# Dealing the first chunk's q and k by groups of heads from two weight halves, and packing attention output two heads a transfer

## The chip, the cores and the metric

One core of one Trainium2 chip runs the kernel. The metric is device time in microseconds (us): the median of three runs was 587.67 (585.95 to 587.77). A separate, profiled execution took 589.12 and left the trace that is read here.

## The reference, cut to what matters

`x` is 2048 rows of 576 numbers (bf16). It is normalised row by row, and two branches are added to it:

```python
xn = _layernorm(x)
# A: sliding-window attention, 32 heads of 18, each query sees itself and the 255 keys before it
qkv = (xn @ wqkv).reshape(B, S, 3, 32, 18)
o = softmax(mask(q @ k.T * 18 ** -0.5)) @ v
a = o.reshape(B, S, 576) @ wo
# B: gated feed-forward, 4608 wide
b = (silu(xn @ w1) * (xn @ w3)) @ w2
out = x + a + b
```

## The kernel before, in words

**Chunks and units.** The 2048 rows are worked in four chunks of 512 (loop at L869). A chunk has a projection stage (q, k and v of its rows), a first phase of 36 *units*, and a second phase that multiplies by w2 and wo and stores the result. Unit u (`unit_pairs` L691, `unit_tanh` L706, `unit_h` L712) makes 128 columns of the gated feed-forward with 18 matmuls (L700), a tanh on ScalarE (L709) and two operations on VectorE (L715, L718). Between the units' matmuls lie the attention's score steps (`scores` L589, `exps` L601, `masks` L608), and three times in a chunk a `pv` (L634) that multiplies the exponentials by v for two groups of heads; the fourth `pv` lies in the second phase. A group is four heads; there are eight groups. TensorE's instructions are in one written order, so a unit whose weights are late holds up all that follows it.

**Weights by fills.** The columns of w1 and w3 come in *fills*: fill k holds 512 columns, serves four units, and is six transfers of 192 KB (`load_part` L314, its DMA L325). There are three buffers, and fill 3 goes into a part of `hT` that is not in use yet. Unit 4 of the first chunk needs all of fill 1, unit 8 all of fill 2, unit 12 fill 3, unit 16 fill 4, unit 20 fill 5, unit 32 fill 8. `load_w13` (L330) issues six transfers at once. `owed` is a debt of transfers: `owe_part` (L337) pays one of them after the fourth and one after the ninth pair of matmuls of a unit, and that transfer waits for the matmul just issued. So a debt of six made before unit u is paid in units u to u+2. w2 comes through `load_w2` (L345, DMA L352).

**The queue of SyncE (SP).** Nearly all transfers are issued by SP, in program order: x tiles (L301), weights (L325, L352), the moves that deal q and k (L527 in the first chunk, L555 later), the attention output (L685), wo (L994, L996) and the results (L766). A transfer that waits for something holds up all that is written after it in this queue. ScalarE (ACT) issues a few transfers as well.

**Dealing q and k.** A projection leaves q and k with columns of the weight matrix on the partitions, 128 to a row tile of `stage` (nine tiles). The score matmuls want, for each group of four heads, two pairs of heads on partitions 0 to 35 and 64 to 99, in `qv` and `kv`. DMAs do this move. From the second chunk on the weights in `wp` are dealt by groups beforehand: row tile g holds the 72 q columns and 54 of the 72 k columns of group g, the remaining 18 k columns of seven groups lie in tile 8, and those of one group in rows 126 and 127 of all tiles. `repack_span` (L532) then moves several groups with one transfer: two for q, three for k, and one for each group's remainder (two for the spread group). In the first chunk the projection uses the weights as they stand in memory (`wa`, which lies over the buffers `pt`; `w8` is a copy of some of its columns): q and k columns in order, so that a head may cross from one tile to the next. `pieces` (L487) cuts every group at the tile borders, and `repack` (L505, DMA L527) issues six to nine transfers for one group alone. Groups 0 and 1 go out while the projections run (`issue_first`, L848), each with a whole fill behind it (fills 1 and 2); the others are issued one group at a time after the projections and in units 1, 6 and 9 on SP (L988), and the last three groups transfer by transfer on ACT and SP's queues (`aside`, L864; L990).

**Start.** x, the v weights and the q and k weights are loaded at L771 to L792; the q and k weights' rows 0 to 511 are one transfer with 2304 contiguous bytes a row (L791). GpSimd (POOL) clears `va`, `qv` (L825) and `kv` (L826), makes the masks and only then deals `wp` with four copies (L844), for the second chunk.

**Attention output.** After a `pv` its output is turned and scaled (`pv_out`, `o_scale`), turned again into a buffer `od` for each group (`o_turn` L671), and `o_pack` (L677, DMA L685) puts each head's 18 rows into `oT` in the order of wo's rows, cut at multiples of 128: four or five transfers for a group, nine for the two groups of a `pv`. The packs of a `pv` in unit u are issued after units u+2 and u+4. wo is loaded in two transfers after unit 25.

Of the kernel before, what the change touches and what calls it, by code (L numbers as in the profile page):

```python
# [164 lines left out]
def bass_parallel_sum__sliding_block__glu_gated_swiglu__prompt_kernel(  # L165
# [32 lines left out]
    with ExitStack() as es:  # L198
# [4 lines left out]
        NXP, NOF, NPT, NW13, NW2, NOD = 7, 4, 10, 3, 4, 3  # L203
# [26 lines left out]
        w8 = pt[:, 6, :, :].rearrange("p q r -> p (q r)")[:, 0:640].rearrange("p (k c) -> p k c", c=128)  # L230
        wa_keys = ["wqk"] + [("pt", n) for n in range(6)]
# [25 lines left out]
        od = [sb(f"od{i}", [128, CH]) for i in range(NOD)]  # L257
# [147 lines left out]
        def pair_of(c, i):  # L405

            return (i, 4 + i) if c == 0 else ((8, 0), (1, 2), (3, 4), (5, 6))[i]

        def proj_part(c, what, banks, part, behind=()):
# [3 lines left out]
            for n in range(5 - part):  # L413
                for r in range(2):
# [4 lines left out]
                    if kind == "q":  # L419
                        t = pair_of(c, i)[x]  # L420
                        st = wp[rows, kd, t, :] if c else wa[rows, kd, x * D + i * 128:x * D + i * 128 + 128]
                        mv = xnT[rows, c % 2, kd, :]
                        keys = (["wp"] if c else wa_keys) + xk(c)
                    elif kind == "8":
                        out_ = PS[:, banks[x], 0:CH // 2]
                        st = wp[rows, kd, i, :] if c else w8[rows, kd, :]
                        mv = xnT[rows, c % 2, kd, x * (CH // 2):(x + 1) * (CH // 2)]
                        keys = (["wp"] if c else ["w8", ("pt", 6)]) + xk(c)
# [58 lines left out]
        def pieces(c0, length):  # L487

            out_ = []
            o = 0  # L490
            while o < length:
                t, r0 = divmod(c0 + o, 128)
                if t < 4:
                    n = min(length - o, 128 - r0)
                    out_.append((t, 4 + t, r0, r0, o, n))
                else:
                    n = length - o
                    out_.append((8, 8, r0, 64 + r0, o, n))
                o += n
            return out_  # L500

        def tiles_of(g):
            return {t for pc in pieces(4 * Dh * g, 4 * Dh) for t in pc[:2]}

        def repack(c, g, eng, q_eng=None):  # L505
            for issue in repack_moves(c, g, eng, q_eng):
                issue()

        def repack_moves(c, g, eng, q_eng=None):

            reads = st_keys(*sorted(tiles_of(g)))
            moves = []
            for pr in range(2):
                for tq, _, rq, _, o, n in pieces(Dh * (4 * g + 2 * pr), 2 * Dh):
                    moves.append((("q", g), qv[64 * pr + o:64 * pr + o + n, g, :], stage[rq:rq + n, tq, :]))
                for p in range(2):
                    for _, tk, _, rk, o, n in pieces(Dh * (4 * g + 2 * pr + p), Dh):
                        p0 = 64 * pr + Dh * p + o
                        moves.append((("k", g), kv[p0:p0 + n, g, :, KB * p:KB * p + KB],
                                      stage[rk:rk + n, tk, :].rearrange("p (b f) -> p b f", f=KB)))  # L520
            seen = set()
            for key, dst, src in moves:
                kw = {"j" if key in seen else "w": [key]}
                seen.add(key)
                by = q_eng or eng if key[0] == "q" else eng
                yield lambda by=by, dst=dst, src=src, kw=kw, key=key: add(
                    by, lambda e: e.dma_start(dst, src), r=reads, dma=f"{key[0]}_{g}", **kw)  # L527

# [3 lines left out]
        def repack_span(a, b, eng, q_eng=None):  # L532

            moves = []
            gs_ = list(range(a, b))
            for pr in range(2):
                moves.append(("q", gs_, gs_, qv[64 * pr:64 * pr + 2 * Dh, a:b, :], stage[2 * Dh * pr:2 * Dh * (pr + 1), a:b, :]))
            for i in range(3):
                r0 = 4 * Dh + i * Dh
                moves.append(("k", gs_, gs_, keys_of(a, b, 64 * (i // 2) + Dh * (i % 2), Dh, i % 2), stage[r0:r0 + Dh, a:b, :].rearrange("q g (b f) -> q (g b) f", f=KB)))  # L540
            p0 = 64 + Dh
            for g in gs_:
                if g < G - 1:
                    moves.append(("k", [g], [8], keys_of(g, g + 1, p0, Dh, 1),
                                  stage[g * Dh:(g + 1) * Dh, 8, :].rearrange("q (b f) -> q b f", f=KB)))
                else:
                    for r in range(2):
                        moves.append(("k", [g], range(9), kv[p0 + r:p0 + r + 2 * 9 - 1:2, g, :, KB:2 * KB], stage[126 + r:127 + r, :, :]))
            seen = set()
            for kind, gset, tset, dst, src in moves:  # L550
                keys = [(kind, g) for g in gs_]
                new = [k for k in keys if k not in seen]
                old = [k for k in keys if k in seen]
                seen |= set(keys)
                add(q_eng if kind == "q" and q_eng else eng, lambda e, dst=dst, src=src: e.dma_start(dst, src),  # L555
                    r=st_keys(*tset), w=new, j=old, dma=f"{kind}_{a}")
# [5 lines left out]

        class Groups:

            def __init__(self):
                self.tiles = set()
                self.g = 0

            def got(self, what):
                kind, i = what  # L570
                if kind == "q":
                    self.tiles |= {i, 4 + i}
                elif kind == "8":
                    self.tiles.add(8)
                while self.g < G and tiles_of(self.g) <= self.tiles:
                    self.g += 1
                    yield self.g - 1
# [93 lines left out]
        def o_turn(g, half):  # L671
            i = g % NOD
            c0 = half * (CH // 2)
            add("dve", lambda e: e.transpose(od[i][:, c0:c0 + CH // 2], oq[:, c0:c0 + CH // 2]),  # L674
                r=["oq", "oq0"], **{"j" if half else "w": [("od", i)]})

        def o_pack(g, eng):  # L677
            first = True
            j, p = divmod(g, 2)
            for q in range(4):  # L680
                o = 0
                while o < Dh:
                    kd, p0 = divmod(Dh * (8 * j + 2 * q + p) + o, 128)
                    n = min(Dh - o, 128 - p0)
                    add(eng, lambda e, kd=kd, p0=p0, n=n, q0=32 * q + o: e.dma_start(  # L685
                        oT[p0:p0 + n, kd, :], od[g % NOD][q0:q0 + n, :]),
# [377 lines left out]
```

## Time and profile before

| what | value |
|---|---|
| median of three runs | 587.67 us |
| profiled execution | 589.12 us, of which the span from first to last instruction is 587.2 us |
| mean granted TensorE clock over the span | 0.988 of full speed |
| TensorE matmul busy | 563.4 us |
| VectorE, ScalarE, GpSimd busy | 315.8, 254.8 and 164.7 us |
| moved by DMA | 83.88 MB |

How to read the rows: times are us from the start of the span; a timeline row gives start, length, engine, source line, operation, output and inputs, and in brackets the idle time of the engine before it and what ended that. "SPq" and "ACTq" rows are the issuing of transfers: the time that SP's or ACT's queue was held by it. In tables by stretch, PEclk is the clock that TensorE was granted, and the DMA share is the mean busy share of the 16 DMA engines. In the list of DMA issues the last number is the median time from issue to landing.

### The profile page before, as it was taken

What the parts mean: (1) busy time and instruction counts of PE and PEld (TensorE: products, weight loads), DVE (VectorE), ACT (ScalarE), POOL (GpSimd) and SP (SyncE); (2) the same over time, 40 slices, a digit from 0 to 9 for tenths busy, and PEclk for the clock granted to TensorE, in tenths of its full rate; (3) what the DMA queues carried; (4) which work ended last, traced back from release to release, by engine and by line L of the source; (5) the groups of instructions that cost most, each with busy time, mean ns of one, the idle gap of its engine ahead of it and who ended that gap; (6) DMA issues with size and microseconds to landing.
All of it is one profiled execution on the core that took longest, in us unless ns stands there. A gap on an engine that the chain in (4) does not pass through costs nothing.

```text
span 587.2 us, 16036 instructions
## 1 busy us (share of the span) xinstructions
PE 563.4 (96%) x6885; PEld 345.9 (59%) x6885; DVE 315.8 (54%) x595; ACT 254.8 (43%) x350; POOL 164.7 (28%) x381
## 2 busy tenths in 40 slices
PE   8985989699999999999999999999999999999998
PEld 3542544367766555547776555656776654554776
DVE  6473668551037787873114878876103567767311
ACT  4343546430017676670005667764001766666000
POOL 6531333330003334352000434454000234434000
PEclk9998989999999999999999999999999999999999
DMA  8746556977535655558653675476653663661452
GB/s 249 168 111 139 121 135 162 216 180 197 151 95 137 146 128 151 133 145 202 163 139 73 133 173 135 121 189 148 173 150 99 139 142 100 140 143 51 114 155 66
DMA packets 119372, 83.88 MB, mean 143 GB/s; under 512 B 26878, under 2 KB 117718, under 8 KB 119302
## 3 DMA queue, kind: packets, MB, share of 16 engines
q1 hardware_dynamic: 115911, 80.45, 55.9%
q10 hardware_dynamic: 3391, 2.41, 1.7%
q8 instruction: 54, 0.88, 0.7%
q14 instruction: 16, 0.13, 0.1%
HBM read 71.29 MB, written 2.36 MB: 125 GB/s over the span
## 4 chain that ended last, share of the span: by engine, by line
PE 88%; DMA 6%; SPq 3%; DVE 1%; issue 1%; ACT 1%; POOL 0%
PE ps L700 44%; PE ps L751 22%; PE ps L434 9%; PE ps L595 5%; DMA w<-in_B_w_dram 5%; PE ps L652 3%; PE ps L757 3%; SPq L527 2%; DMA hT<-in_B_w_dram 1%; SPq L325 1%; ACT xnT L391 0%; DMA xp<-in_A_x_dram 0%; PE ps L384 0%; DVE gs L715 0%; DVE hT L718 0%
## 5 line engine op out<-in xcount | busy, mean ns | idle before, releaser
L700 PE MATMUL ps<-xnT,w 64*128 64x512 bf16 x1400 | 185.8, 378 | 10.3 <-DMA w<-in_B_w_dram 10.3
L700 PE MATMUL ps<-xnS,w 64*128 64x512 bf16 x1120 | 155.6, 379 | 0.0
L715 DVE SCALAR_TENSOR_TENSOR gs<-th,ps 128x512 bf16<-128x512 bf16 x144 | 97.9, 680 | 97.5 <-ACT th L709 96.7
L604 ACT ACTIVATE pt<-ps 128x1024 bf16<-128x1024 f32 (+1 forms) x112 | 113.1, 1010 | 85.8 <-PE ps L595 85.5
L751 PE MATMUL ps<-w,hT 128*128 128x288 bf16 x1152 | 147.5, 286 | 1.7 <-DMA w<-in_B_w_dram 1.7
L751 PEld LDWEIGHTS ps<-w,hT 128*128 128x128 bf16 x1152 | 111.8, 98 | 32.7 <-DMA w<-in_B_w_dram 2.5
L700 PEld LDWEIGHTS ps<-xnT,w 64*128 64x128 bf16 x1400 | 70.2, 94 | 66.8 <-DMA w<-in_B_w_dram 8.7
L631 POOL TENSOR_TENSOR pt<-pt,mk 128x128 int32<-128x128 int32 (+1 forms) x199 | 80.9, 429 | 96.1 <-ACT pt L604 95.9
L718 DVE SCALAR_TENSOR_TENSOR hT<-gs,ps 128x512 bf16<-128x512 bf16 x144 | 98.9, 687 | 5.0
L709 ACT ACTIVATE th<-ps 128x512 bf16<-128x512 f32 x144 | 85.5, 594 | 27.4 <-PE ps L700 26.8
L700 PEld LDWEIGHTS ps<-xnS,w 64*128 64x128 bf16 x1120 | 58.5, 94 | 54.0 <-issue 1.3
L764 DVE TENSOR_TENSOR ofin<-ps,xp 128x288 bf16<-128x288 f32 x32 | 14.6, 458 | 121.8 <-PE ps L757 121.8
L447 ACT ACTIVATE stage<-ps 128x512 bf16<-128x512 f32 x16 | 9.6, 597 | 147.8 <-PE ps L434 145.5
L631 POOL TENSOR_TENSOR hT<-hT,mk 128x128 int32<-128x128 int32 (+1 forms) x31 | 12.5, 424 | 159.6 <-ACT hT L604 159.6
L595 PE MATMUL ps<-qv,kv 64*128 64x320 bf16 (+4 forms) x528 | 54.3, 262 | 0.0
L595 PEld LDWEIGHTS ps<-qv,kv 64*128 64x128 bf16 x528 | 28.1, 95 | 26.4 <-issue 1.6
L434 PE MATMUL ps<-xnT,wp 64*128 64x512 bf16 (+1 forms) x270 | 29.5, 355 | 0.0
L674 DVE STREAM_TRANSPOSE od<-oq 128x256 bf16<-128x256 bf16 x64 | 25.8, 427 | 6.3 <-POOL oq L667 6.3
L604 ACT ACTIVATE stage<-ps 128x1024 bf16<-128x1024 f32 x24 | 24.5, 1023 | 10.2 <-PE ps L595 10.1
L667 POOL TENSOR_TENSOR oq<-uq,rden 128x288 bf16<-128x288 f32 x16 | 10.8, 672 | 54.5 <-DVE rden L666 54.5
L757 PE MATMUL ps<-wo,oT 128*128 128x288 bf16 x160 | 24.8, 286 | 0.0
L434 PE MATMUL ps<-wv,xnT 64*128 64x288 bf16 x288 | 21.7, 283 | 0.8 <-ACT xnT L391 0.7
(62 smaller groups left out, 367.2 us busy)
## 6 DMA issues: line engine op xcount, KB each, us to landing
w<-in_B_w_dram SPq DMA_DIRECT2D x210, 192.0 KB, 4.0
w<-in_B_w_dram SPq DMA_DIRECT2D x72, 288.0 KB, 3.2
xp<-in_A_x_dram SPq DMA_DIRECT2D x29, 144.0 KB, 3.1
out_dram<-ofin SPq DMA_DIRECT2D x32, 72.0 KB, 1.6
oT<-od SPq DMA_DIRECT2D x84, 18.0 KB
xnS<-xnT SPq DMA_DIRECT2D x5, 256.0 KB, 5.3
pt<-in_A_wqkv_dram SPq DMA_DIRECT2D x1, 1152.0 KB, 9.2
hT<-in_B_w_dram SPq DMA_DIRECT2D x6, 192.0 KB, 3.6
```

Of the source, the lines that this page charges most:

```text
L434: op = add("pe", lambda e, out_=out_, st=st, mv=mv, n=n, r0=r0, first=first: e.matmul(out_, st, mv, start=first, stop=(part == 1 and n == ...
L595: add("pe", lambda e, r0=r0, out_=out_, kb=kb, q0=q0, nb=nb: e.matmul(out_, kb4[r0:r0 + 64, g, kb + NV - NB, :] if kb < 0 else kv[r0:r0 + ...
L604: add("act", lambda e: e.activation(pt_slot(sl)[:, 0:w, :], PS[:, SC[0]:SC[1] + 1, 0:w].rearrange("p r q -> p q r"), ACT.Exp, scale=scale) ...
L631: add("pool", lambda e, vb=vb, mm=mm: e.tensor_tensor(vb, vb, mm, ALU.mult), r=(key if n == 0 else []) + ["mk"], **{"w" if n == 0 else "j" ...
L652: add("pe", lambda e, p=p, q=q, pr=pr, sl=sl, g=g, pos=pos, q0=q0, nb=nb, col=col, first=first, n=n: e.matmul(PS[32 * q:32 * q + VW, banks ...
L674: add("dve", lambda e: e.transpose(od[i][:, c0:c0 + CH // 2], oq[:, c0:c0 + CH // 2]), r=["oq", "oq0"], **{"j" if half else "w": [("od", i)]})
L700: op = add("pe", lambda e, n=n, r0=r0, r=r, k=k, src=src: e.matmul(PS[:, b0 + r, :], wt[r0:r0 + 64, k, fl * 128:(fl + 1) * 128], src, star ...
L709: add("act", lambda e: e.activation(th[i][:], PS[:, bg, :], ACT.Tanh, scale=0.5), r=[("ps", bg)], w=[("th", i)])
L715: add("dve", lambda e: e.scalar_tensor_tensor(out=gs[i][:], in0=th[i][:], scalar=1.0, in1=PS[:, bg, :], op0=ALU.add, op1=ALU.mult), r=[("t ...
L718: add("dve", lambda e: e.scalar_tensor_tensor(out=hT[:, u, :], in0=gs[i][:], scalar=0.5, in1=PS[:, bu, :], op0=ALU.mult, op1=ALU.mult), r= ...
L751: add("pe", lambda e: e.matmul(bank, hT[:, f, tt * 128:(tt + 1) * 128], w2[sl][:, k, :], start=(f == 0), stop=False), r=[("h", f), ("w2", ...
L757: add("pe", lambda e: e.matmul(bank, oT[:, k, tt * 128:(tt + 1) * 128], wo[:, k, d0:d0 + HD], start=False, stop=(k == 4)), r=[("oT", g) fo ...
```

## The change

The first chunk uses the dealt weights as the others do.

- The q and k weights come in two column halves: columns 0 to 287 of q and of k (heads 0 to 15, groups 0 to 3) are two transfers, columns 288 to 575 another two, with 576 contiguous bytes a row. The last 64 rows come through ACT's queue.
- GpSimd deals `wp` at once when a half has landed, with four copies for the first half and three for the second; its clears are moved around that (`qv` to VectorE at the start; `kv` in two parts), and the projection's first weights are now `wp`, tiles 0 to 3 needing the first half only.
- `pieces`, `repack`, `Groups`, `aside` and `w8` go. Groups 0 and 1 are moved with `span_main(0, 2)` after the first projection of q and k and `span_last(0, 2)` after the third, which has tile 8; behind these, two x tiles and fill 1. Groups 2 to 7 are moved at the end of unit 1 with one `repack_span(2, 8)`. Fill 2 is no longer loaded at once: the debt made at unit 0 is twelve transfers instead of six.
- The spread group is number 3 instead of 7.
- `od` holds two groups; `o_pack` moves one head of both groups with one transfer, four for a `pv` (six for the last), after unit u+3. `oT` has seven heads, 126 rows, to a row tile; wo is loaded to match it, in five transfers after unit 13, and the rows left over are cleared in units 8 to 11.

```diff
-        def repack_span(a, b, eng, q_eng=None):
+        def span_main(a, b, q_eng="sp"):
+            gs_ = list(range(a, b))
             moves = []
...
+            for pr in range(2):
+                moves.append(("q", q_eng, gs_, qv[64 * pr:64 * pr + 2 * Dh, a:b, :], stage[2 * Dh * pr:2 * Dh * (pr + 1), a:b, :]))
             for i in range(3):
                 r0 = 4 * Dh + i * Dh
...
+                moves.append(("k", "sp", gs_, keys_of(a, b, 64 * (i // 2) + Dh * (i % 2), Dh, i % 2),
+                              stage[r0:r0 + Dh, a:b, :].rearrange("q g (b f) -> q (g b) f", f=KB)))
+            span_issue(a, b, moves, True)
+        def span_last(a, b):
...
+            for g in sorted(range(a, b), key=lambda g: g == SPREAD):
+                if g != SPREAD:
+                    r0 = (g - (g > SPREAD)) * Dh
+                    moves.append(("k", "sp", [8], keys_of(g, g + 1, p0, Dh, 1),
+                                  stage[r0:r0 + Dh, 8, :].rearrange("q (b f) -> q b f", f=KB)))
...
         def o_turn(g, half):
-            i = g % NOD
+            i = g // 2 % NOD
...
-        def o_pack(g, eng):
+        def o_pack(j, eng):
+            i = j % NOD
             first = True
...
+            for q in range(4):
+                m = 4 * j + q
+                if m < 14:
+                    t, r0 = 2 * (m // 7), Dh * (m % 7)
+                    moves = [(oT[r0:r0 + Dh, t:t + 2, :], od[i][32 * q:32 * q + Dh, :, :])]
...
+        for h in range(2):
+            for n in range(2):
+                c0 = n * D + h * HD
+                add("sp", lambda e, c0=c0: e.dma_start(
+                    wa[:, 0:4, c0:c0 + HD], A_wqkv[0:512, c0:c0 + HD].rearrange("(kd p) f -> p kd f", p=128)),
+                    dma=f"wqk{h}", **{"j" if n else "w": [f"wqk{h}"]})
         for p in range(2):
...
+            add("act", lambda e, p=p: e.dma_start(
+                wa[64 * p:64 * p + 64, 4, :], A_wqkv[512:576, 0:2 * D]), dma="wqkd", **{"j" if p else "w": ["wqkd"]})
...
+        for h in range(2):
+            a, b = 4 * h, 4 * h + 4
+            moves = [(wpf[:, :, a:b, 0:2 * Dh], wf[:, :, 0, a:b, :]),
+                     (wpf[:, :, a:b, 2 * Dh:7 * Dh // 2], wf[:, :, 1, a:b, 0:3 * Dh // 2])]
...
+            for n, (dst, src) in enumerate(moves):
+                dealt.append(add("pool", lambda e, dst=dst, src=src: e.tensor_copy(dst, src),
+                                 r=[f"wqk{h}", "wqkd"], **{"j" if n else "w": [f"wp{h}"]}))
...
-        for what in [("q", 0), ("q", 1), ("q", 2), ("q", 3), ("8", 8), None]:
+        for what in [("q", 0), ("q", 1), ("q", 2), ("q", 3), ("8", 7), None]:
             got = proj_begin(0, what) if what else proj_end()
-            for g in groups.got(got):
-                issue_first(0, g)
-        repack(0, held.pop(0), "sp")
...
+            if got == ("q", 0):
+                span_main(0, 2, "act")
+            elif got == ("q", 2):
+                span_last(0, 2)
+                for t in (TB, TB + 1):
+                    xslot[t] = load_x(t)
+                load_w13()
...
                 if c == 0 and u == 0:
-                    owed += 6
+                    owed += 12
...
-                    later(u + 2, lambda j=j: (o_turn(2 * j + 1, 0), o_pack(2 * j, "sp")))
-                    later(u + 3, lambda j=j: o_turn(2 * j + 1, 1))
-                    later(u + 4, lambda j=j: o_pack(2 * j + 1, "sp"))
+                    later(u + 2, lambda j=j: o_turn(2 * j + 1, 0))
+                    later(u + 3, lambda j=j: (o_turn(2 * j + 1, 1), o_pack(j, "sp")))
...
-                if c == 0 and u in (1, 6, 9):
-                    repack(0, held.pop(0), "sp")
...
+                if c == 0 and u == 1:
+                    repack_span(2, G)
```

More of the change, by code (lines that the diff above doesn't have):

```diff
@@ L546, in repack_span @@
                 else:
                     for r in range(2):
[L548 to L556, printed above, removed]
+                        moves.append(("k", "sp", range(9), kv[p0 + r:p0 + r + 2 * 9 - 1:2, g, :, KB:2 * KB], stage[126 + r:127 + r, :, :]))
```

200 lines of the change are left out of this document (69 added, 131 removed).

## The prediction, made before the changed kernel had run

> **What bounds the kernel now.** First the page's line of busy time, then TensorE's waits, then TensorE's timeline at the places of those waits.
>
> ```profile
> PE 563.4 (96%) x6885; PEld 345.9 (59%) x6885; DVE 315.8 (54%) x595; ACT 254.8 (43%) x350; POOL 164.7 (28%) x381
> ```
>
> ```profile
> PE ps L751 <- DMA w<-in_B_w_dram: 1.7, 2, 0.9
> ```
>
> ```profile
> 42.19 1.04 PE L700 MATMUL ps<-xnT,w 64*128 64x512 bf16 x8 [2.57 <-DMA w<-in_B_w_dram]
> ...
> 57.30 1.04 PE L700 MATMUL ps<-xnT,hT 64*128 64x512 bf16 x4 [6.42 <-issue]
> ...
> 80.04 1.04 PE L700 MATMUL ps<-xnT,w 64*128 64x512 bf16 x8 [2.43 <-DMA w<-in_B_w_dram]
> ...
> 115.67 1.89 PE L700 MATMUL ps<-xnT,w 64*128 64x512 bf16 x8 [5.31 <-DMA w<-in_B_w_dram]
> ```
>
> TensorE is the bound: of 587.2 us it is idle for 23.8. Four stalls of the first chunk hold 2.57 + 6.42 + 2.43 + 5.31 = 16.73 of these, each before the first matmul of a unit whose fill is late: units 8, 12, 20 and 32 (fills 2, 3, 5, 8). Two waits of the second phase, in the second and third chunk, hold 1.7 more. Chunks two to four otherwise run without a gap, so the change has to earn its time in the first chunk.
>
> A stall also costs clock afterwards. The table by stretches, around the last three stalls:
>
> ```profile
> 57.30:60.80 3.50, 3.50 (x20) 1.64 (x22) 0.00 (x0) 0.00 (x0) 0.00 (x0) 0.50 1.11 227
> 81.28:84.70 3.42, 3.42 (x77) 1.82 (x80) 0.65 (x1) 1.51 (x2) 0.74 (x2) 0.50 0.93 187
> 110.40:115.67 5.27, 0.00 (x0) 0.03 (x1) 3.02 (x7) 1.30 (x2) 1.36 (x3) 0.98 1.14 231
> 115.67:118.83 3.16, 3.16 (x16) 1.36 (x18) 0.00 (x0) 0.00 (x0) 0.00 (x0) 0.50 1.11 258
> ```
>
> The third last column is the granted clock. After stalls two, three and four TensorE works at half speed for 3.50, 3.42 and 3.16 us, which loses half of each: 1.75, 1.71 and 1.58 us. The first stall cost no clock. Together the stalls of the first chunk cost 16.73 + 5.04 = 21.8 us.
>
> Why are the fills late? SP's timeline from the first dealt group to fill 2:
>
> ```profile
> 17.94 3.49 SPq L527 DMA_DIRECT2D kv<-stage  x4
> 21.47 4.98 SPq L325 DMA_DIRECT2D w<-in_B_w_dram  x6
> 26.49 1.07 SPq L301 DMA_DIRECT2D xp<-in_A_x_dram  x2
> 27.67 0.84 SPq L527 DMA_DIRECT2D qv<-stage  x1
> 28.55 1.65 SPq L527 DMA_DIRECT2D kv<-stage  x2
> 30.24 1.44 SPq L527 DMA_DIRECT2D qv<-stage  x2
> 31.72 2.28 SPq L527 DMA_DIRECT2D kv<-stage  x3
> 34.04 4.47 SPq L325 DMA_DIRECT2D w<-in_B_w_dram  x6
> ```
>
> SP issues back to back. A transfer holds its queue for 0.6 to 0.9 us, whatever it carries, and the landing follows by the list of issues, whose first row here is w1 and w3 and whose second is w2:
>
> ```profile
> w<-in_B_w_dram SPq DMA_DIRECT2D x210, 192.0 KB, 4.0
> w<-in_B_w_dram SPq DMA_DIRECT2D x72, 288.0 KB, 3.2
> ```
>
> Fill 2's last transfer goes at about 37.8, and 4 us later unit 8 starts. So **SP's queue of issues, in program order, is the limit of the first chunk**, and the change must be costed in that queue.
>
> **The change part by part. What is removed.** These rows are SP's own issues by source line (least, median, largest ns), and the chain's piece of the last stall:
>
> ```profile
> L527 SPq DMA_DIRECT2D kv<-stage x27: 649/782/996, 17.9 to 74.1; - x27
> L527 SPq DMA_DIRECT2D qv<-stage x13: 597/791/869, 27.7 to 72.4; - x13
> ```
>
> ```profile
> L685 SPq DMA_DIRECT2D oT<-od x108: 559/735/1375, 81.1 to 539.5; - x108
> ```
>
> ```profile
> 106.61 8.16 DMA w<-in_B_w_dram
> ```
>
> Dealing costs SP 40 issues in the first chunk; after the change 5 (three main, two remainders) and 12, that is 17. Packing costs 108 / 4 = 27 in a chunk; after it 12. wo costs three more. So 35 issues of about 0.78 us, some 27 us, leave SP's queue before the end of the first phase, and the ACT queue loses its share too, which hides nothing.
>
> **What is moved.** Fill 2 goes behind the one block of twelve. The same shape of block exists in the second chunk, eleven issues with up to five groups in one:
>
> ```profile
> 185.15 1.67 SPq L555 DMA_DIRECT2D qv<-stage  x2
> 186.87 8.51 SPq L555 DMA_DIRECT2D kv<-stage  x9
> ```
>
> These took 10.23 us, 0.93 each; at the median of single-group issues (0.79) twelve would take 9.5, at this rate 11.2. I take 10.7. Now SP's queue after the change, on today's clock. It needs the time of the third projection's copy to `stage`, and ScalarE's unit ends:
>
> ```profile
> 21.11 0.69 DVE L446 CAST stage<-ps 128x512 bf16<-128x512 f32 x1 [1.25 <-PE ps L434]
> ```
>
> ```profile
> 26.81 0.60 ACT L709 ACTIVATE th<-ps 128x512 bf16<-128x512 f32 x1 [1.34 <-PE ps L700]
> ...
> 31.14 0.60 ACT L709 ACTIVATE th<-ps 128x512 bf16<-128x512 f32 x1 [0.36 <-PE ps L700]
> ```
>
> Three main k moves from 17.94 end at 20.6 (q's two go by ACT, as group 0's do today). The remainders wait for tile 8, copied at 21.11 + 0.69 = 21.8; two of them end at 23.5, two x tiles (1.1) at 24.6, fill 1 (5.0) at 29.6. Four transfers of fill 2 follow (0.65 each, 32.2), since units 0 and 1 are past by then; the block of twelve ends at 42.9, fill 2's last two at 44.2. The last is issued at 43.5 and lands 4.0 later, **47.5**.
>
> TensorE: unit 1 to unit 3 ends by 31.14 − 26.81 = 4.33, so 2.17 a unit, and unit 4 wants fill 1 at 31.2. Its last transfer now goes at 29.0 instead of 25.8 and lands at about 33.2: a new stall of 2 us. Unit 8 would be reached at 33.2 + 4 × 2.17 = 41.9 and starts at 47.5: a stall of 5.6 us in place of 2.57. The first is swallowed by the second, so what counts is that unit 8 starts 47.5 − 42.19 = **5.3 us later** than today. Of the half-speed stretches I take the mean, 1.7 us, after this stall (0.5 to 2.5, as an idle time of 5.6 is between the 5.31 and 6.42 that had one).
>
> After unit 8 the queue has caught up: fill 3's six issues end at 48.1 and land by 52.1, unit 12 is reached at 47.5 + 1.7 + 8.7 = 57.9. Fill 5 is paid in units 9 to 11 and wanted in unit 20. So **stalls two and three go**: 6.42 + 1.75 + 2.43 + 1.71 = 12.31. Fill 8 is paid in units 24 to 26. The pack after unit 23 now stands directly behind its turn on VectorE, so SP waits there about 2.5 us (tanh 0.60, two products of 0.69, a turn) and issues four (3.1): fill 8 can be 5.6 us behind its due time, and has 5 units, 11 us, less 4 us of landing. **Stall four goes** as well, 5.31 + 1.58 = 6.89, as wo's bytes are also gone from there. The two waits of the second phase (1.7) follow packs that stand late in SP's queue ahead of w2; with one pack fewer I take **1.7** saved, between 0 and 1.7.
>
> **The start.** Today the projection reads the weights as they land; now GpSimd's copies lie between.
>
> ```profile
> 3.60 0.46 DVE L360 BATCH_NORM_STATS2 stats<-xp 128x6 f32<-128x288 bf16 x1 [2.41 <-DMA xp<-in_A_x_dram]
> ```
>
> ```profile
> 4.24 0.59 SPq L791 DMA_DIRECT2D pt<-in_A_wqkv_dram  x1
> ```
>
> ```profile
> 15.05 7.84 PE L434 MATMUL ps<-xnT,pt 64*128 64x512 bf16 x80
> ```
>
> ```profile
> 19.22 3.27 POOL L844 COPY wp<-pt 128x1440 f32<-128x1440 f32 x4
> ```
>
> ```profile
> pt<-in_A_wqkv_dram SPq DMA_DIRECT2D x1, 1152.0 KB, 9.2
> ```
>
> The whole block lands at 4.24 + 9.2 = 13.4. The first half then lands about 2.6 us before (half of 1152 KB at the 231 GB/s of the 110.40 row), 10.8, and its share of the four copies, 1.7, is done at 12.5, before the first q matmuls at 13.4. The second lands at 13.4 and is dealt by 15.0; it is first wanted by the third projection, which begins after 18 of the 80 matmuls, 15.05 + 1.8 = 16.9. So the deal is hidden with 1.9 us to spare, and costs 0. Rows of 576 bytes are w2's too, and those land no later than w1's of 1024 bytes (3.2 against 4.0 us); if the second half's 2.6 us doubled all the same, as the landing at 106.61 did, its deal would end at 17.6, 0.7 too late, and all of the queue would move by that. I keep 0 to 0.7.
>
> VectorE's clear of `qv` has eight times the 256 words of this one:
>
> ```profile
> 0.91 0.27 DVE L779 MEMSET oq<- 128x256 f32 x1 [0.91 <-PEq L1049]
> ```
>
> By its 0.27 that is 2.2 us, inside the 2.41 us that VectorE idles before its first statistics; without that cover it would cost its length. By the same rate the two larger clears of units 8 and 10 take 1.2 us each beside a unit's 1.4 of VectorE work in 2.17; they lie behind the stall of unit 8, and cost at most the 0.4 us by which they overflow.
>
> [...]
>
> **Sum.** −5.3 − 1.7 + 12.31 + 6.89 + 1.7 = 13.9 us gained. The profiled execution's 589.12 would become 575.2; it stands 1.45 above the median of the runs, so I predict 587.67 − 13.9 = **573.8**, for this case 570 to 577.
>
> **The rivals.**
>
> *The last stall is one of data, not of issues.* For it: the DMA share of the 110.40 row is 1.14, and the chain's piece at 106.61 took 8.16 us to land, twice the median. Against it: those transfers were issued some four units late, and the pile of wo, x and w2 around them came from SP's delay. If it stays, 6.89 is not earned: 580.7. [...]
>
> *Unit 8 is not held.* If the block of twelve costs SP so little that fill 2 is issued by 37.9 (41.9 − 4.0), 5.6 us earlier than I reckon, all 21.8 and 1.7 are earned: 564.2. Against it: that is 0.43 us an issue, below the least of the rows (559 ns).
>
> *The change doesn't do what it says.* If an issue is held in proportion to the rows that it carries, the block costs as much as the pieces did and SP is no earlier: 587. Against it: the L555 rows.
>
> *Slower: the pack's new wait.* In every chunk SP now stops at the pack until VectorE has done the turn just written, with w1 and w3 transfers behind. I reckon 5.6 us; a part has 6 units, 13.0, less 4.0 of landing, so it decides from 9.0 us of stop. Beyond that each of nine packs in chunks two to four stalls TensorE and costs a half-speed stretch, 0.2 + 1.7: 17.1 us lost against 13.9 gained, 590.9. Against it: the waits of those chunks today are 1.7 us in all.
>
> **How the numbers follow.** Forecast 0.66; stall four stays 0.14; unit 8 not held 0.08; no effect 0.05; slower 0.07. A measurement here can tell about 0.3%, 1.8 us, from no change. Faster by more: 0.66 + 0.14 + 0.08 = 0.88; within: 0.05; slower: 0.07. The range 568 to 583 takes in the forecast's bounds (the start's 0.7, the second phase's 1.7, the half-speed stretch, 0.8 of the block) and the first rival, and leaves the others out.
>
> **What would show it.** Right: about 17 dealing issues of SP in the first chunk, at 0.8 to 0.9 us each; TensorE idle for about 2 us before unit 4 and 5 to 6 before unit 8, with one half-speed stretch after it; no idle time from unit 9 to the second phase; no wait of L751. Wrong: an idle time before the third projection (the deal is on the path), a stall before unit 28 or 32, or SP's rows growing with the rows carried.

## The result and the profile after

| what | before | changed |
|---|---|---|
| median of four runs each | 587.20 us (585.95 to 587.77) | 579.66 us (579.13 to 581.27) |
| profiled execution, its span | 589.12, 587.2 us | 579.13, 577.4 us |
| mean granted TensorE clock | 0.988 | 0.991 |

The ratio is 0.9879, with a 95% interval of 0.9853 to 0.9906: 7.5 us faster by the medians, where 13.9 was predicted. The forecast's own time was 573.8, and its case reached from 570 to 577; the time lies above that, inside the range of 568 to 583.

Busy time, from the page of the changed kernel. TensorE is idle for 577.4 − 560.2 = 17.2 us, where it was 23.8:

```profile
PE 560.2 (97%) x6885; PEld 334.6 (58%) x6885; DVE 319.6 (55%) x598; ACT 254.1 (44%) x349; POOL 163.2 (28%) x384
```

TensorE's timeline at the places where it waits for weights (the brackets give the idle time before the row):

```profile
32.53 0.61 PE L654 MATMUL ps<-xnT,w 64*128 64x512 bf16 x4 [1.15 <-DMA w<-in_B_w_dram]
...
49.26 1.89 PE L654 MATMUL ps<-xnT,w 64*128 64x512 bf16 x8 [8.03 <-DMA w<-in_B_w_dram]
...
126.08 0.66 PE L705 MATMUL ps<-w,hT 128*128 128x288 bf16 x4 [1.06 <-DMA w<-in_B_w_dram]
```

L654 is the units' matmul, which was L700, and L705 that of the second phase, which was L751. The four stalls before units 8, 12, 20 and 32 have become two: 1.15 us before unit 4, and one of 8.03 before unit 8. The stretches show the clock around the long one; the third last column is the granted clock:

```profile
43.58:53.82 10.24, 4.57 (x26) 2.08 (x28) 0.76 (x3) 0.93 (x2) 0.72 (x2) 0.50 0.78 173
...
49.26:53.82 4.56, 4.56 (x26) 2.05 (x28) 0.00 (x0) 0.93 (x2) 0.00 (x0) 0.50 1.10 230
53.82:577.40 523.58, 518.73 (x6470) 313.94 (x6466) 290.12 (x536) 234.27 (x319) 142.54 (x339) 1.00 0.58 142
```

After the stall TensorE works at half speed for 4.56 us and loses 2.28; from 53.82 to the end it has its full clock. Now SP's queue in the first chunk, in the order of its program:

```profile
18.23 5.48 SPq L492 DMA_DIRECT2D kv<-stage  x5
...
24.90 6.62 SPq L323 DMA_DIRECT2D w<-in_B_w_dram  x10
31.57 1.66 SPq L492 DMA_DIRECT2D qv<-stage  x2
33.27 11.65 SPq L492 DMA_DIRECT2D kv<-stage  x10
44.96 1.36 SPq L323 DMA_DIRECT2D w<-in_B_w_dram  x2
46.37 3.87 SPq L323 DMA_DIRECT2D hT<-in_B_w_dram  x6
```

The block of twelve takes from 31.57 to 44.92, 13.35 us. The ten k moves (to `kv`) alone take 11.65, and the chain of work that ended last shows which of them took it (start, length):

```profile
33.27 0.81 SPq L492
...
34.12 1.09 SPq L492
...
35.25 3.32 SPq L492
...
38.61 1.40 SPq L492
```

The first three are the wide moves, each of six groups: the third held the queue for 3.32 us, and the remainder behind it for 1.40. The other six took 0.77 to 0.80. Fill 2's last two transfers, issued behind the block, landed 3.5 us after their issue, no later than the 4.0 that is usual in the kernel before. They were late because they were issued late.

### The profile page after: what moved, and what is told of

The parts are those of the page before. It is cut to its first block, busy times and chain, and to the rows that moved or that the text cites. A ratio compares the mean times of both kernels' runs of the same rounds, so it can differ in the third digit from the quotient of the medians.

```text
span 577.4 us, 15920 instructions
## 1 busy us (share of the span) xinstructions
PE 560.2 (97%) x6885; PEld 334.6 (58%) x6885; DVE 319.6 (55%) x598; ACT 254.1 (44%) x349; POOL 163.2 (28%) x384
## 4 chain that ended last, share of the span: by engine, by line
PE 91%; DMA 3%; SPq 2%; DVE 2%; issue 1%; ACT 1%; POOL 0%
PE ps L654 45%; PE ps L705 24%; PE ps L430 9%; PE ps L547 6%; PE ps L604 3%; PE ps L711 3%; SPq L492 2%; DMA w<-in_B_w_dram 2%; DMA wv<-in_A_wqkv_dram 1%; DVE hT L672 0%; DVE gs L669 0%; ACT xnT L389 0%; PE ps L382 0%; ACT th L663 0%; DVE wo L948 0%
## 5 line engine op out<-in xcount | busy, mean ns | idle before, releaser
L654 PE MATMUL ps<-xnT,w 64*128 64x512 bf16 x1400 | 183.3, 378 | 9.2 <-DMA w<-in_B_w_dram 9.2
L654 PE MATMUL ps<-xnS,w 64*128 64x512 bf16 x1120 | 152.6, 378 | 0.0
L705 PE MATMUL ps<-w,hT 128*128 128x288 bf16 x1152 | 147.4, 286 | 1.1 <-DMA w<-in_B_w_dram 1.1
L705 PEld LDWEIGHTS ps<-w,hT 128*128 128x128 bf16 x1152 | 111.9, 98 | 31.9 <-DMA w<-in_B_w_dram 1.7
L654 PEld LDWEIGHTS ps<-xnT,w 64*128 64x128 bf16 x1400 | 65.8, 94 | 68.8 <-DMA w<-in_B_w_dram 10.1
L654 PEld LDWEIGHTS ps<-xnS,w 64*128 64x128 bf16 x1120 | 54.8, 94 | 55.8 <-issue 0.8
L583 POOL TENSOR_TENSOR hT<-hT,mk 128x128 int32<-128x128 int32 (+1 forms) x31 | 12.5, 425 | 162.7 <-ACT hT L556 162.7
L547 PE MATMUL ps<-qv,kv 64*128 64x320 bf16 (+4 forms) x528 | 51.7, 261 | 1.0 <-issue 0.7
L547 PEld LDWEIGHTS ps<-qv,kv 64*128 64x128 bf16 x528 | 25.9, 95 | 29.1 <-issue 1.5
L430 PE MATMUL ps<-xnT,wp 64*128 64x512 bf16 (+1 forms) x360 | 38.3, 355 | 0.0
L430 PEld LDWEIGHTS ps<-xnT,wp 64*128 64x128 bf16 x360 | 17.4, 94 | 15.6 <-issue 0.7
```

The lines of the kernel that those rows point to most:

```text
L430: op = add("pe", lambda e, out_=out_, st=st, mv=mv, n=n, r0=r0, first=first: e.matmul(out_, st, mv, start=first, stop=(part == 1 and n == ...
L547: add("pe", lambda e, r0=r0, out_=out_, kb=kb, q0=q0, nb=nb: e.matmul(out_, kb4[r0:r0 + 64, g, kb + NV - NB, :] if kb < 0 else kv[r0:r0 + ...
L583: add("pool", lambda e, vb=vb, mm=mm: e.tensor_tensor(vb, vb, mm, ALU.mult), r=(key if n == 0 else []) + ["mk"], **{"w" if n == 0 else "j" ...
L654: op = add("pe", lambda e, n=n, r0=r0, r=r, k=k, src=src: e.matmul(PS[:, b0 + r, :], wt[r0:r0 + 64, k, fl * 128:(fl + 1) * 128], src, star ...
L705: add("pe", lambda e: e.matmul(bank, hT[:, f, tt * 128:(tt + 1) * 128], w2[sl][:, k, :], start=(f == 0), stop=False), r=[("h", f), ("w2", ...
```

## The experiments

Two readings of what held unit 8 stood against each other. **The theory**: SP's queue, in program order. Fill 2's last two transfers stand behind the block, so unit 8 starts when the block is through, and what matters is where a block stands relative to the fill that is wanted next. **The rival**: the data, that is, the moves and the weights are in each other's way in the DMA engines, and the fill would be late wherever it is issued. Beside these, the size of each term was open. All diffs are against the changed kernel and cut to what matters (`...`). The kernel before ran on the same chip in each group; its median was 589.16 us beside the first four, 588.39 beside the next four and 588.06 beside the last three. The changed kernel's own ratio was 0.9879 at first and 0.9870 in the second group; it wasn't run beside the first four. Spans below are compared with its one profile.

| kernel | median us | ratio to before | 95% interval |
|---|---|---|---|
| block one unit later | 576.74 | 0.9796 | 0.9767 to 0.9826 |
| TensorE kept busy | 578.05 | 0.9818 | 0.9785 to 0.9851 |
| wide moves apart | 578.54 | 0.9820 | 0.9792 to 0.9847 |
| pack one unit later | 577.40 | 0.9808 | 0.9778 to 0.9838 |
| dealing alone | 582.14 | 0.9899 | 0.9880 to 0.9918 |
| packing alone | 580.71 | 0.9871 | 0.9854 to 0.9889 |
| block in three pieces at three places | 567.26 | 0.9647 | 0.9629 to 0.9666 |
| changed kernel again | 579.99 | 0.9870 | 0.9846 to 0.9893 |
| three pieces, and 64 weight rows on SP | 565.88 | 0.9619 | 0.9590 to 0.9647 |
| three pieces at the block's place | 585.71 | 0.9965 | 0.9947 to 0.9983 |
| block issued by GpSimd | 583.65 | 0.9923 | 0.9894 to 0.9952 |

**The block one unit later.** Units 0 to 2 then pay the whole debt of twelve before the block.

```diff
-                if c == 0 and u == 1:
+                if c == 0 and u == 2:
                     repack_span(2, G)
```

> One edit of the changed kernel: the block of twelve dealing transfers is issued at the end of unit 2 instead of unit 1, so that the last two transfers of fill 2 stand ahead of it in SP's queue; nothing else. Order-of-the-queue theory: fill 2 lands by 37, unit 8 starts when it is reached (about 41 instead of 49.3), the 8.0 us of idle time and the half-speed stretch there go; fill 3 is still behind the block and lands at about 54.3, so a new stall of 4 us stands before unit 12, with a half-speed stretch of about 1.7. Unit 12 is 5 us earlier in all: 574.6 us. Rival, the fills wait for the DMA engines' data and not for their place in the queue: the same bytes are moved in the same time, no change, 579.7.

SP's queue, then TensorE's timeline and the stretch behind the stall:

```profile
32.93 1.66 SPq L492 DMA_DIRECT2D qv<-stage  x2
34.64 12.74 SPq L492 DMA_DIRECT2D kv<-stage  x10
```

```profile
55.16 1.89 PE L654 MATMUL ps<-xnT,hT 64*128 64x512 bf16 x8 [4.30 <-DMA hT<-in_B_w_dram]
```

```profile
55.16:59.86 4.70, 4.70 (x26) 2.10 (x28) 0.00 (x0) 1.06 (x2) 0.00 (x0) 0.51 1.13 236
```

The stall before unit 8 is gone and fill 3 (in `hT`) is late instead, by 4.30 us before unit 12, with half speed behind it. Fill 2, issued ahead of the block, came in time: the order in the queue decides. The span is 574.5, 2.9 below that of the changed kernel: the block, 14.45 us here, was only put ahead of the next fill. By the ratios (0.9796 against 0.9879 and 0.9870) the gain is some 4 to 5 us.

**TensorE kept busy.** 36 matmuls on zeros before unit 8, which add work and change no result of the others.

```diff
+                if c == 0 and u == 8:
+                    warm(b0[0], 36)
```

> One edit of the changed kernel: 36 matmuls of 512 columns on zeros (0.216 us each, 7.8 us) into the PSUM bank that unit 8 overwrites, ahead of unit 8, so that TensorE is not idle while it waits for fill 2. Theory: the stall is as long as before, but no half-speed stretch follows; 4.56 us at half speed lose 2.28, so 577.4. Rival, the half speed is hidden, as VectorE or ScalarE set the pace of the first units after a stall: no change, 579.7.

```profile
42.85 7.72 PE L738 MATMUL ps<-oq 128*128 128x512 bf16 x35 [0.16 <-issue]
50.50 1.04 PE L654 MATMUL ps<-xnT,w 64*128 64x512 bf16 x8
```

```profile
50.50:52.60 2.10, 2.10 (x25) 1.07 (x26) 0.00 (x0) 0.15 (x1) 0.00 (x0) 1.00 1.12 231
```

Unit 8's first 25 matmuls take 2.10 us at full clock, where 26 took 4.56 at half: that loss of about 2.3 us is real and goes when TensorE is kept busy through the wait. The span is only 0.9 shorter (576.5). Unit 8 starts at 50.50 instead of 49.26; the block began 1.23 us later in this run too (32.80 against 31.57), since unit 0's tanh came at 26.56 instead of 25.16.

**The wide moves apart.** The same twelve transfers in another order: one wide k move, one of q, three remainders, and so on.

```diff
-                    repack_span(2, G)
+                    repack_apart(2, G)
...
+            span_issue(a, b, [wide[0], q[0], *rest[0:3], wide[1], q[1], *rest[3:6], wide[2], *rest[6:]], True)
```

> One edit of the changed kernel: the same twelve dealing transfers in another order, the three wide k moves (48 x 18 pieces of 128 bytes) apart with three or four narrow ones between them instead of one behind the other. Backlog theory (an issue is held when the transfers ahead of it have too many pieces outstanding): the third wide issue is no longer held for 3.3 us nor the next for 1.4, the block takes 9.7 to 10.5 us instead of 13.4, fill 2 lands 3 us earlier, 576.7. Rival, a wide transfer costs its issue in itself: the same 13.4 us, 579.7.

```profile
33.12 0.84 SPq L492 DMA_DIRECT2D kv<-stage  x1
34.00 1.56 SPq L492 DMA_DIRECT2D qv<-stage  x1
35.60 3.25 SPq L492 DMA_DIRECT2D kv<-stage  x4
38.90 1.86 SPq L492 DMA_DIRECT2D qv<-stage  x1
40.80 4.12 SPq L492 DMA_DIRECT2D kv<-stage  x5
```

The block takes 11.8 us instead of 13.35. No k move is held now; the two q transfers are, by 1.56 and 1.86 us, each right behind a wide k move. So a hold falls on what follows a wide k move, and the order alone takes 1.55 us off the block, of the 3.9 by which it exceeds twelve times the median of 0.79. The stall before unit 8 is 6.49; the span falls by only 0.5, since this run lost 1.4 us at its start (unit 0's tanh at 26.55). By the ratios (0.9820 against 0.9879 and 0.9870) the gain is about 3 us, as expected; with one profile of each the two aren't brought together.

**The pack one unit later.**

```diff
-                    later(u + 3, lambda j=j: (o_turn(2 * j + 1, 1), o_pack(j, "sp")))
+                    later(u + 3, lambda j=j: o_turn(2 * j + 1, 1))
+                    later(u + 4, lambda j=j: o_pack(j, "sp"))
```

> One edit of the changed kernel: the pack of a pair of groups is issued one unit later, after u+4 instead of u+3, when VectorE's turn has long been done. Theory: SP no longer stops about 2.5 us before each pack; in the first chunk the reload of w2 is issued 2 us earlier and the wait of 1.06 us in the second phase goes: 578.6. Rival, the pack's four issues now stand nearer to the second phase and delay w2 as much or more: 579.7 to 581.

SP's queue near the end of the first chunk, in the changed kernel and then here:

```profile
109.81 0.59 SPq L323 DMA_DIRECT2D w<-in_B_w_dram  x1
112.94 0.79 SPq L641 DMA_DIRECT2D oT<-od  x1
```

```profile
108.14 4.03 SPq L323 DMA_DIRECT2D w<-in_B_w_dram  x4
112.57 3.09 SPq L641 DMA_DIRECT2D oT<-od  x4
```

In the changed kernel SP stands still from 110.40 to 112.94 at the pack, waiting for the turn; here 0.4 us. The wait of 1.06 at L705 is gone, and the span is 574.7, 2.7 less: 1.06 of it from there, 0.38 from unit 8, which starts at 48.88 here, and 0.8 from TensorE's waits at L547 (the scores), 0.98 before and 0.2 here. Why those shrank, and the remaining half microsecond, isn't shown.

**Each part alone.** Dealing as changed with the packing of before, and the other way round. Of each diff only the places of the issues are shown; the rest of the part (`od`, `oT` and wo in the one, all of the first chunk's dealing in the other) is as before too.

```diff
...
-                    later(u + 2, lambda j=j: o_turn(2 * j + 1, 0))
-                    later(u + 3, lambda j=j: (o_turn(2 * j + 1, 1), o_pack(j, "sp")))
+                    later(u + 2, lambda j=j: (o_turn(2 * j + 1, 0), o_pack(2 * j, "sp")))
+                    later(u + 3, lambda j=j: o_turn(2 * j + 1, 1))
+                    later(u + 4, lambda j=j: o_pack(2 * j + 1, "sp"))
...
```

> One part of the change alone: the first chunk dealt by groups from two halves, with the packing of before (one group a transfer, nine transfers for a pair of groups, wo in two transfers after unit 25). Theory: the backlog of SP's queue came from the pieces, so without them stalls three and four stay away although the packing is the old one; the stall before unit 8 is that of the full change (8.0 us and a half-speed stretch). The two waits of the second phase in chunks two and three (0.77 and 0.90) come back, that of 1.06 in the first goes: 580, a ratio of 0.988 to before. Rival, stall four was the packs' and wo's: 5.3 + 1.6 us return, 586.5.

```diff
...
-                if c == 0 and u == 1:
-                    repack_span(2, G)
+                if c == 0 and u in (1, 6, 9):
+                    repack(0, held.pop(0), "sp")
...
```

> The other part alone: packing two heads a transfer and wo in five transfers after unit 13, with the first chunk dealt by pieces as before. Theory: stalls one to three (2.57, 6.42, 2.43 us with 3.46 lost at half speed) stay, as they lie ahead of the packs; 18 packs become 8 ahead of fill 8 and wo's bytes are gone from there, so fill 8 is about 5 us earlier and stall four (5.31 + 1.58) goes: 580, a ratio of 0.988; the two parts' gains then do not add up, since both remove stall four. Rival, packing is off the path: 587, ratio 1.0.

Dealing alone, at unit 32; its block of twelve ends at 45.17, with fill 2's last two transfers behind it at 45.21, and it also waits 1.41 at the start of the first chunk's second phase:

```profile
108.78 1.04 PE L652 MATMUL ps<-xnT,w 64*128 64x512 bf16 x8 [1.51 <-DMA w<-in_B_w_dram]
```

Packing alone, the stall before unit 8; 4.04 before unit 12 and 2.28 before unit 20 followed, and none before unit 32:

```profile
42.17 1.76 PE L702 MATMUL ps<-xnT,w 64*128 64x512 bf16 x8 [2.61 <-DMA w<-in_B_w_dram]
```

Both parts work on the last stall: dealing cuts 5.31 to 1.51, packing ends it. So the gains don't add. Packing alone gives all that the whole change gives (0.9871 against 0.9870 in the same group). Dealing, placed as it is, earns stalls two and three and spends them before unit 8.

**The block in three pieces, each ahead of a fill that has time.** Groups 2, 3 to 4 and 5 to 7 are moved after units 2, 5 and 11: 22 transfers instead of twelve. Two of fill 1's transfers go ahead of the remainders of groups 0 and 1 and the other four ahead of the x tiles; the pack stands one unit later, as above (not shown again).

```diff
...
                 span_main(0, 2, "act")
+                for _ in range(2):
+                    load_part()
             elif got == ("q", 2):
                 span_last(0, 2)
+                for _ in range(4):
+                    load_part()
...
-                load_w13()
...
-                if c == 0 and u == 1:
-                    repack_span(2, G)
+                if c == 0 and u in (2, 5, 11):
+                    repack_span(*{2: (2, 3), 5: (3, 5), 11: (5, G)}[u])
```

> The changed kernel with three edits that the theory asks for: the block of twelve is cut in three by need (group 2 after unit 2, groups 3 and 4 after unit 5, groups 5 to 7 after unit 11; 22 transfers in all, so ten more than the block), two of fill 1's transfers go ahead of the remainders of groups 0 and 1 into the time in which SP waits for tile 8, the x tiles behind fill 1, and the pack one unit later. Theory: SP has time enough for more transfers if no fill stands behind dealing that is not needed yet: no stall in the first phase, no half-speed stretch, none of the 12.5 us that these cost the changed kernel: 567, a ratio of 0.966. Rival, the number of issues counts: ten more hold fills 4 to 6 up, 579 or more.

```profile
28.36 3.88 SPq L323 DMA_DIRECT2D w<-in_B_w_dram  x6
32.28 1.65 SPq L492 DMA_DIRECT2D qv<-stage  x2
33.98 3.27 SPq L492 DMA_DIRECT2D kv<-stage  x4
37.30 3.97 SPq L323 DMA_DIRECT2D hT<-in_B_w_dram  x6
```

The six transfers of fill 2 (first row) go out before the first piece, the six of fill 3 before the second. No wait for a fill is left, the clock is 1.0 over the whole span, and 567.26 us is 12.7 less than the changed kernel in the same group. By the changed kernel's rows 1.15 + 8.03 + 2.28 + 1.06 = 12.5 us were to be had. Ten transfers more, and 12.7 us less.

**The changed kernel again**, in the same group:

> The changed kernel once more without any edit, on the same chip as the three others, to have its ratio beside theirs: 0.988 again, 8.0 us of idle time before unit 8.

Six runs gave 579.46 to 583.73; the profiled one is the slowest of them, and stalls 8.6 us before unit 8.

**Is it the place or the size of the pieces?** The same three pieces, all where the block stood:

```diff
-                    repack_span(2, G)
+                    for ab in ((2, 3), (3, 5), (5, G)):
+                        repack_span(*ab)
```

> The changed kernel with the block cut in the same three pieces as in e7 (22 transfers), but all three left at the end of unit 1. Against e7 this holds the transfers' number and widths and undoes their places. Place theory: 22 issues at about 0.8 and less holding behind the wide ones take 17.6 to 19 us instead of 13.4, fill 2 lands 4 to 6 us later still, unit 8 starts at about 54: 584 to 586. Rival, the width of the moves was what cost: narrower moves, a shorter block, 577 or less.

```profile
32.10 1.67 SPq L492 DMA_DIRECT2D qv<-stage  x2
...
45.28 4.88 SPq L492 DMA_DIRECT2D kv<-stage  x6
50.21 1.34 SPq L323 DMA_DIRECT2D w<-in_B_w_dram  x2
```

```profile
54.49 1.89 PE L654 MATMUL ps<-xnT,w 64*128 64x512 bf16 x8 [12.36 <-DMA w<-in_B_w_dram]
```

The 22 transfers take 18.1 us, 0.82 each, with no hold; unit 8 starts at 54.49 behind a stall of 12.36. So smaller pieces are not what helped: in the block's place they make it longer. The same pieces gave 567.26 apart. That kernel also has fill 1's transfers earlier and the pack one unit later, so not all of the 18.4 us between the two are the place. But 1.62 + 12.36 us of stalls before units 4 and 8 and 2.8 lost at half speed make 16.8 of them, and the one-edit run above showed that moving the block alone moves such a stall. What fill 1's order is worth by itself was not run.

**The block issued by GpSimd**, so that SP has none of it. If issuing were all, fill 2 would be early.

```diff
...
-                    repack_span(2, G)
+                    span_main(2, G, "pool", "pool")
+                    span_last(2, G, "pool")
```

> The changed kernel with the block of twelve issued from GpSimd's queue instead of SP's, at the same place in the program. Theory: with the block out of SP's way fill 2 lands by 37 and the 8.0 us before unit 8 and the half-speed stretch go; if GpSimd issues the twelve in less than about 12 us, group 2's scores near unit 10 do not wait: 569 to 570. Rival: GpSimd is slower at issuing than SP, and its masks stand behind the transfers; then a wait of that size stands before the scores of group 2 near unit 10 or the product with v near unit 13, 575 or more. No row so far shows an issue by GpSimd.

GpSimd's timeline, SP's, a stretch and TensorE's:

```profile
25.73 1.34 POOL L492 DMA_DIRECT2D qv<-stage  x2 [5.49 <-DVE stage L446]
27.07 7.08 POOL L492 DMA_DIRECT2D kv<-stage  x10
```

```profile
26.07 14.45 SPq L323 DMA_DIRECT2D w<-in_B_w_dram  x12
```

```profile
32.00:36.00 4.00, 0.71 (x8) 0.10 (x3) 2.96 (x7) 0.86 (x2) 3.85 (x9) 1.00 1.16 125
```

```profile
43.93 1.04 PE L654 MATMUL ps<-xnT,w 64*128 64x512 bf16 x4 [11.21 <-DMA w<-in_B_w_dram]
```

The theory missed by 14 us, and the rival's 575 or more came true by a wait that it didn't name. GpSimd issues the twelve in 8.4 us, but now they meet fill 1: from 32 to 36 the DMA share is 1.16 at 125 GB/s, where the changed kernel has 1.05 at 230, SP's twelve weight transfers hold its queue for 1.20 us each instead of 0.65, and unit 4 waits 11.21 us. Unit 8 isn't held. So the rival has its case as well: with the moves issued this way, the weights that are in flight with them are late (11.53 us from issue to landing for the one that unit 4 waited for, by the chain, against a median of 4.0). Whether the moves do this when SP issues them, no run shows. A block of 13.35 us leaves SP's queue, but the saving is lost again in the wait for fill 1.

**The best version.** The three pieces, with the last 64 rows of the q and k weights between the halves on SP again.

```diff
-        for p in range(2):
-            add("act", lambda e, p=p: e.dma_start(
...
+            for p in range(2 - 2 * h):
+                add("sp", lambda e, p=p: e.dma_start(
...
```

> The kernel cut in three (e7) with one more edit: the last 64 rows of the q and k weights go back to SP's queue, behind the first half's two transfers, instead of ACT's queue ahead of the v weights' landing. The changed kernel's first v projection waits 0.4 to 1.0 us for the v weights, which the kernel before did not. Theory: that wait goes and unit 0 is 0.5 us earlier: 566.7, at the limit of what can be told; the trace's first 15 us tell it. Rival: the wait stays, as it comes from the halves behind it in the same queue: 567.3.

The first v matmuls with the three pieces, and here:

```profile
8.21 0.79 PE L430 MATMUL ps<-wv,xnT 64*128 64x288 bf16 x10 [1.00 <-DMA wv<-in_A_wqkv_dram]
```

```profile
7.49 0.79 PE L430 MATMUL ps<-wv,xnT 64*128 64x288 bf16 x10
```

The wait for the v weights is gone and the kernel takes 565.88 us, ratio 0.9619: the fastest of all, 1.4 us below the other. How much of that 1.4 is the edit isn't settled, as starts differ from run to run.

## Why the prediction was partly right

**Right.** SP's queue in program order is the limit: the block moved by one unit moved the long stall from fill 2 to fill 3, and the same 22 dealing transfers gave 585.71 us in one place and, with two smaller edits, 567.26 in three. Stalls two, three and four went, 6.42 + 1.75 + 2.43 + 1.71 + 5.31 + 1.58 = 19.2 us. A new short stall came before unit 4 (1.15 against 2), a longer one before unit 8, and one half-speed stretch. The deal at the start is hidden:

```profile
10.36 1.81 POOL L798 COPY wp<-pt 128x720 f32<-128x720 f32 x4 [0.67 <-DMA pt<-in_A_wqkv_dram]
12.61 1.65 POOL L798 COPY wp<-pt 128x720 f32<-128x720 f32 x3 [0.44 <-DMA pt<-in_A_wqkv_dram]
```

```profile
13.77 1.24 PE L430 MATMUL ps<-xnT,wp 64*128 64x512 bf16 x10
...
15.34 7.84 PE L430 MATMUL ps<-xnT,wp 64*128 64x512 bf16 x80
```

The first half is dealt by 12.2, before the first q matmuls at 13.77. The second is dealt by 14.3, before the third projection, which begins after 18 of the eighty that start at 15.34. These have no idle time before them, so nothing of the 0.7 us that the prediction allowed for a late deal shows.

**What was mis-sized.** The step that failed is "I take 10.7" for the block. It took 13.35, and unit 8 started 49.26 − 42.19 = 7.07 us later than before instead of 5.3 (0.29 of it from the start: unit 1's tanh at 27.10 against 26.81). Part of the 2.65 us was won back: the block began at 31.57, not 32.2, and fill 2 landed 3.5 us after its issue, not 4.0. The working divided a block's time by its number of transfers, and in that average a hold was hidden that is one transfer's own. The rows of before had it, in the largest value of its dealing from the second chunk on:

```profile
L555 SPq DMA_DIRECT2D kv<-stage x54: 786/809/2531, 171.0 to 474.1; - x54
```

A largest value of three times the median asks for a look at which transfer has it: the last of three wide ones in a row, in each of the three chunks (1.61, 2.14 and 2.53 us). With six groups instead of five it held 3.32. SP's rows growing with what they carry was one of the prediction's own signs of being wrong; it showed in the three rows from the second wide move to the first remainder (1.09, 3.32 and 1.40), and nowhere else in the block.

The half-speed stretch lost 2.28 instead of 1.7: that is near the top of the 0.5 to 2.5 that the prediction allowed. In the second phase 1.7 was counted as saved, and it is saved, but a new wait of 1.06 came in the first chunk; 0.6 is left. It goes when the pack is issued a unit later, so the pack's stop on SP, which the fourth rival describes, takes part in it. It isn't the only cause: dealing alone, with the packing of before, waits 1.41 there. Two waits of 0.28 and 0.70 at L547 weren't foreseen.

The sum of the trace is so −7.07 − 2.28 + 19.20 + 0.61 − 0.98 = 9.5 us, beside a span that fell by 9.8. The medians differ by 7.5 only, because before's profiled execution stood 1.92 above its four runs' median and the changed one's 0.53 below. That is the rest of the distance to 13.9: 4.4 us of terms, and about 2 of executions. In the repeat, beside eleven runs of the kernel before, the medians differ by 8.4.

**The rivals.** That the last stall is one of data doesn't hold: dealing alone, with wo still loaded after unit 25, cut it to 1.51. What ended the rest with the packing, fewer issues or wo's bytes gone from there, isn't told apart. That unit 8 isn't held is false as the change stands, and true of the three pieces, which at 567.26 come near that rival's 564.2, though not by its reason of cheap issues. That the change does nothing, or that the pack's wait makes it slower, is false; the pack's wait exists, though: SP stands still for 2.5 us at the pack before that wait of 1.06.

## What to carry to other kernels

Where one queue issues everything in program order, cost a block of transfers by what is written behind it: merging transfers into one large block can lose to more and smaller ones that each stand behind a fill that was paid in time (579.99 us against 567.26 here, with two smaller edits beside it). Cost such a block from its rows one by one, with the largest value and its place, not from the mean. When two parts of a change work on the same stall, price each alone: the sum counts that stall twice.

## What the runs showed of the hardware that was not expected

**Wide moves hold the queue behind them.** A dealing transfer of one group holds SP for about 0.8 us; the third of three wide ones in a row 3.32, a wide q move right behind a wide k move 1.56 and 1.86. In the first chunk no piece of one to three groups was held (22 transfers at 0.82 us each in the block's place). Why was not tried.

**The length of the idle time alone does not decide whether the clock drops.** With packing alone TensorE was granted half speed after 2.61 us of idle time before unit 8 and full speed after 2.28 before unit 20:

```profile
42.30:45.70 3.40, 3.40 (x22) 1.63 (x20) 0.38 (x2) 0.03 (x1) 0.34 (x1) 0.51 0.20 34
...
80.90:84.00 3.10, 3.03 (x86) 1.84 (x94) 0.09 (x1) 1.09 (x2) 0.00 (x0) 1.00 0.64 180
```

In the kernel before it was the other way round: full speed after 2.57 at the one place, half after 2.43 at the other. The stretches between two changes of the clock are whole multiples of 3.41 us in both profiles: in before half speed for 6.83 from 53.98, 3.41 from 81.28 and 3.41 from 115.42, with 20.48 and 30.72 at full speed between them, in the changed kernel half speed for 10.24. By an estimate that carries steps of 3.41 on from these times, the idle time of 2.43 leaves TensorE only 1.24 us of work in the step that ends at 81.28; that of 2.57 falls on two steps and leaves them 2.70 and 1.55. With packing alone it is 0.80 where the clock fell and some 2.2 and 2.3 where it stayed. So in these four places the clock fell where a step had the least work; no run varied it.

**The start differs from run to run.** Unit 0's tanh in the changed kernel and in its repeat:

```profile
25.16 0.60 ACT L663 ACTIVATE th<-ps 128x512 bf16<-128x512 f32 x1 [1.79 <-PE ps L654]
```

```profile
26.23 0.60 ACT L663 ACTIVATE th<-ps 128x512 bf16<-128x512 f32 x1 [1.79 <-PE ps L654]
```

1.07 us apart with the same program. Two other runs started as late, with slower matmuls at the start: TensorE's first ten v matmuls, 0.79 us in the first profile, take 1.38 in the run with TensorE kept busy (unit 0's tanh at 26.56) and 1.36 in that with the wide moves apart (at 26.55), where the granted clock is 0.51 from 8.0 to 11.4 instead of 1.00. Whether the repeat's start was slow in the same way isn't shown. So a single profile can't size an effect of one microsecond; the comparisons above that are smaller than that rest on the rows of the stall itself.
